# A GLA-plus-mixer kernel with a hand-written instruction order: another order and another buffer assignment

## The chip, the cores and the metric

The kernel runs on one core of one Trainium2 chip. The metric is the device time of one execution in microseconds. All times below are of that kind, or are spans and durations out of one profiled execution.

## The reference

Two layers follow each other. The first is a gated linear recurrence over 768 positions for 4 batches and 8 heads of width 48; the second is a mixer over tokens and then over channels, on the 4 x 768 x 384 result. Inputs and output are float32.

```python
for t in range(S):                      # S = 768, D = 48
    state = alpha[:, :, t, :, None] * state + einsum('bhd,bhe->bhde', k[:, :, t], v[:, :, t])
    y[:, :, t] = einsum('bhd,bhde->bhe', q[:, :, t], state)
x = y.transpose(0, 2, 1, 3).reshape(B, S, H * D)          # 4 x 768 x 384
h = maximum(x.transpose(0, 2, 1) @ w_tok1, 0) @ w_tok2    # 768 -> 256 -> 768
u = x + h.transpose(0, 2, 1)
out = u + maximum(u @ w_ch1, 0) @ w_ch2                   # 384 -> 1536 -> 384
```

## The kernel before

**The recurrence** is cut into twelve pieces n = 0 to 11 of 256 positions, three per batch (n = 3b + k). A piece holds its positions as 128 partitions x 2 slots, for all heads. Per piece: four loads of 384 KB (`ld_at` alpha, `ld_kt`, `ld_qt`, `ld_vt`); the logarithm of alpha (`ln`, from n = 3 on split in `P`, `ln1`, `lnP`, `r1`); its running sum by matmuls with a triangle (`cum`, `cumw`); the exponentials `E` and `IE`; the scaled keys and queries (`kk`, `kl` = keys x IE into `pkk`; `qq`, `ql` = queries x E into `pkq`, with `k0a` and `q0r` ahead of them from n = 3 on); a bf16 copy of v (`vb`) and the swapped halves of it (`vs0`, `vs1`); the transposes of keys and queries (for n < 6 on TensorE, `trk`, `trq`, with copies `evk`, `evq` out of PSUM; for n >= 6 by DMA transposes `dk`, `dq`, and a rearranging copy `pq`); the scores `G0`, `G1` and their masks; the outer products `K`, the state (`s0`, `sa`, `sm`), and the output `ia`, `ib`, `y0`, `y1`, copied out as `x0`, `x1`. From n = 3 on, `K` reads keys whose halves were exchanged between partitions by copies `ka`, `kb` (into `kt`) and `kc` (within `pkk`).

**The mixer** of batch b: `t1` (12 matmuls of 384 columns) and its ReLU `ht`; `t2` (6 groups of 2) and u = x + t2 (`u`); the transpose of u (`up` and copies `ut` on TensorE for batches 0 and 1, DMA transposes `ux` for 2 and 3); the first channel product `c1` (24 groups of 3 matmuls of 384 columns) with 24 ReLUs `rt`; the second, `c2` (6 rows x 4 groups of 3 matmuls), the sum `o` with u, and the store `st`. The 16 weight pieces (`ldw`, 384 KB each) come in on the same SyncE queue as the inputs and are cast to bf16 by `cw`.

**What sets the order.** A `Plan` object holds 946 named operations with what each writes, reads and waits for. A string `ORDER` lists them all, and the letter behind each name is its engine: t TensorE (PE), s ScalarE (ACT), v VectorE (DVE), g GpSimd (POOL), y SyncE (SP). Operations are emitted in the order of that list, so each engine's queue is the list's subsequence with its letter. A second string, `BUFS`, gives each value, when it is first met, a buffer out of its class (20 input buffers `in`, 8 PSUM banks `ps`, 20 `rt`, 4 `o` and so on). Waits follow from this: an instruction waits for its inputs and for the last user of the buffer that it writes.

```python
"in": 20, "la": 2, "lf": 2, "E": 3, "IE": 2, "pkq": 2, "pkk": 3, "vb": 3,
"tpk": 4, "tpq": 2, "gtm": 2, "tmp": 2, "ss": 4, "kt": 1, "x": 9, "ht": 3, "u": 4, "ut": 1, "rt": 20, "o": 4,
```

Operations marked `port` (products and casts between SBUF buffers: `P`, `k0a`, `q0r`, `kk`, `kl`, `qq`, `ql`, `vb`, `vs`, `ka`, `kb`, `kc`, `pq`, `cw`, and `sm` from n = 3 on) take turns between VectorE and GpSimd: where such an operation follows one on the other of the two engines in `ORDER`, it waits for it (function `shared`).

```python
if last and last[0] != e:
    self.tc.add_manual_dep(i.ins, last[1].ins.name, ...)
```

At the start, 25 matmuls on zeros (names `f1_`, `f3_`: one or three of 512 columns) stand ahead of the operation that they are named for. Lines that matter below: L604 recurrence matmuls and fillers, L805 `t1`, L810 `t2`, L821 `up`, L829 `c1`, L834 `c2`; L800 and L802 ReLUs on ACT and DVE; L697 copies on ACT, L698 copies on DVE and POOL; L720 masks; L589 `P`, L645 `k0a`, L649 `q0r`, L653 scaled keys and queries, L771 `sm`; L545 input loads, L677 DMA transposes of keys and queries, L585 stores.

Of the kernel before, what the change touches and what calls it, by code (L numbers as in the profile page):

```python
# [380 lines left out]
vs0_1g f3_G12t G0_2t G1_2t mask0_1v ldw_wt10y vs1_1g sm0_2v cw_wt10g t1_0_0_0t t1_0_0_1t ld_at3y P3g ldw_wt11y
cw_wt11g mask0_2v ia1t y0_1t ib1t t1_0_1_0t y1_1t ia2t lnP3s cum3t t1_0_1_1t y0_2t ld_kt3y x0_1s t1_0_0_2t ib2t
mask1_2v y1_2t ldw_wt20y t1_0_1_2t x1_1s t1_0_0_3t t1_0_1_3t IE3s x0_2v k0a3v t1_0_1_4t ldw_wt21y t1_0_0_4t x1_2s
t1_0_1_5t cw_wt20v ln13s kk3g kl3g t1_0_0_5t ht_0_0s cw_wt21s ht_0_1v t2_0_2t u_0_2v t2_0_1t u_0_1v ld_at4y P4g lnP4s
ldw_wc13y cw_wc13g t2_0_0t t2_0_3t t2_0_4t t2_0_5t u_0_0v up_0_0t ka3g kb3g u_0_3v up_0_1t ldw_wc11y trk3t cum4t
ut_0_1s IE4s E3s r13s E4s u_0_4v u_0_5v up_0_2t ldw_wc10y cw_wc10g ut_0_0v c1_0_7_0t c1_0_6_0t ut_0_2v c1_0_6_1t evk3v
rt_0_6_0s ld_qt3y kc3s cw_wc11v qq3v c1_0_7_1t rt_0_7_1s c1_0_1_0t c1_0_0_0t rt_0_0_0v ln14s r14s ld_vt3y vb3s
c1_0_3_0t c1_0_3_1t c1_0_1_1t c1_0_2_1t c1_0_2_0t q0r3g rt_0_6_1v rt_0_3_1v rt_0_7_0s rt_0_2_0s ql3g trq3t rt_0_3_0s
vs0_3g rt_0_1_1v rt_0_1_0v vs1_3g K3t s0_3v sa1_3v c1_0_0_1t ldw_wc14y cw_wc14g c1_0_8_1t c1_0_8_0t ldw_wc12y evq3s
ld_qt4y G0_3t rt_0_2_1s G1_3t cw_wc12g c1_0_4_0t q0r4g ql4g rt_0_0_1v ldw_wc15y cw_wc15s rt_0_8_1v mask0_3v qq4g  # L390
c1_0_9_1t rt_0_9_1s c1_0_11_1t c1_0_9_0t rt_0_9_0s rt_0_8_0v c1_0_11_0t ld_kt4y mask1_3v kk4g c1_0_5_1t trq4t k0a4v
kl4v c1_0_4_1t c1_0_5_0t rt_0_11_1s rt_0_4_0s ldw_wc20y cw_wc20s ldw_wc21y rt_0_11_0s evq4v trk4t rt_0_4_1s ld_at5y
cw_wc21g c2_0_2_0t P5g sm1_3g ka4g rt_0_5_0s c2_0_4_0t rt_0_5_1s ldw_wc22y kc4g cw_wc22s lnP5s evk4v G1_4t G0_4t
ld_vt4y vb4g mask1_4v ln15s r15s ib3t c1_0_10_0t rt_0_10_0v y1_3t c2_0_4_1t mask0_4v c2_0_2_1t c1_0_10_1t c2_0_1_0t
kb4s vs1_4s ldw_wc24y cw_wc24s vs0_4g x1_3v K4t y0_3t ldw_wc23y x0_3s cum5t IE5s E5s c2_0_1_1t cw_wc23g c2_0_4_2t
sa0_4v sm0_4v sa1_4v ia4t y0_4t ld_at6y ln16s t1_1_0_0t r16s P6g c2_0_1_2t sm1_4v c2_0_2_2t ldw_wc25y cw_wc25v x0_4s
c2_0_0_0t c2_0_0_1t rt_0_10_1s c2_0_4_3t lnP6s cum6t E6s ib4t IE6s ld_qt5y q0r5v qq5v c2_0_2_3t y1_4t x1_4s trq5t
evq5s ld_kt5y k0a5v kk5v o_0_2v c2_0_1_3t o_0_1v ld_vt5y trk5t kc5s evk5v c2_0_0_2t c2_0_0_3t o_0_4v G1_5t ld_at7y
mask1_5v ld_kt7y G0_5t P7g t1_1_0_1t c2_0_5_0t c2_0_5_1t vb5s ld_at8y ld_vt7y ia5t mask0_5v vs0_5s lnP7s ld_kt6y k0a7g
K5t sa0_5v c2_0_5_2t t1_1_0_2t sm0_5v P8g c2_0_5_3t t1_1_1_0t y0_5t t1_1_1_1t x0_5v t1_1_1_2t ib5t vs1_5s y1_5t x1_5s  # L400
c2_0_3_0t t1_1_1_3t t1_1_1_4t st_0_2y t1_1_0_3t t1_1_0_4t t1_1_1_5t t1_1_0_5t ht_1_0s cum7t IE7s c2_0_3_1t ht_1_1v
t2_1_0t u_1_0v t2_1_1t u_1_1v E7s t2_1_2t u_1_2v t2_1_3t u_1_3v c2_0_3_2t t2_1_4t u_1_4v t2_1_5t up_1_0t k0a6g ln17s
# [490 lines left out]
```

## Time and profile before

| | before |
|---|---|
| median of 3 runs | 164.17 us (163.75 to 164.42) |
| profiled execution: its time, its span | 164.12 us, 162.4 us |
| PE busy | 153.8 us (95%), 1598 matmuls |
| DVE busy | 112.4 us (69%), 200 instructions |
| ACT busy | 98.5 us (61%), 184 instructions |
| POOL busy | 80.4 us (50%), 95 instructions |
| HBM read, written | 25.17 MB, 4.72 MB |

The span runs from the first to the last instruction of the profiled execution; its time is 1.7 us longer. Busy time counts a matmul from its start to its modelled end, and matmuls overlap, so a hole in TensorE's row is shorter in the profile than the time that it costs.

### The profile page before, as it was taken

Reading aid. Unit: us, or ns where it says so; the run is one execution under the profiler, and the core shown is the slowest. Engines: PE = TensorE matmul, PEld = TensorE weight load, DVE = VectorE, ACT = ScalarE, POOL = GpSimd, SP = SyncE. Lnnn points to the kernel's source line nnn. Section 1 sums busy time; section 2 is a strip of 40 time slices with the busy share of each in tenths; the row PEclk is TensorE's granted clock in tenths of the full one; section 3 lists DMA queues with packets and bytes.
Section 4 is the critical chain, followed back from the end, with each engine's and each line's share of the span. In section 5 each row is a group of like instructions: output and inputs, shape, how many; then the busy total and the mean of one; then the engine's idle time right before and its main releaser. Section 6 shows DMA issues by size and latency. Waiting matters only on the chain.

```text
span 162.4 us, 4056 instructions
## 1 busy us (share of the span) xinstructions
PE 153.8 (95%) x1598; PEld 97.3 (60%) x1598; DVE 112.4 (69%) x200; ACT 98.5 (61%) x184; POOL 80.4 (50%) x95
## 2 busy tenths in 40 slices
PE   7988798999999999999899999999999999999992
PEld 2556465665666766756556675666667666666661
DVE  4287987988988994958896859767876544551232
ACT  3897576887889774899999794518532101437000
POOL 4066575769694048997279998658320000000000
PEclk9999999999999999999999999999999999999999
DMA  5999999999999999899999999999531063101134
GB/s 135 325 325 304 262 350 358 301 315 359 354 281 259 274 299 326 182 251 224 258 251 166 270 161 311 154 239 246 69 145 52 0 154 77 59 4 48 48 145 145
DMA packets 76322, 34.46 MB, mean 212 GB/s; under 512 B 68112, under 2 KB 76304, under 8 KB 76304
## 3 DMA queue, kind: packets, MB, share of 16 engines
q1 hardware_dynamic: 75152, 32.64, 79.4%
q10 hardware_dynamic: 1152, 1.57, 2.6%
q8 instruction: 12, 0.20, 0.5%
q14 instruction: 6, 0.05, 0.1%
HBM read 25.17 MB, written 4.72 MB: 184 GB/s over the span
## 4 chain that ended last, share of the span: by engine, by line
PE 66%; ACT 10%; DMA 7%; POOL 5%; DVE 5%; issue 4%; SPq 1%; DVEq 0%; POOLq 0%; ACTq 0%
PE ps L834 26%; PE ps L829 19%; PE ps L604 14%; DMA in<-in_alpha_dram 7%; PE ps L805 3%; PE ps L810 3%; ACT rt L800 3%; DVE gtm L720 2%; POOL vb L698 1%; POOL pkk L653 1%; PE ps L666 1%; DVE u L814 1%; SPq L677 1%; POOL in L589 1%; ACT lf L592 1%
## 5 line engine op out<-in xcount | busy, mean ns | idle before, releaser
L834 PE MATMUL ps<-wc,rt 128*128 128x384 bf16 (+2 forms) x300 | 53.2, 319 | 0.0
L829 PE MATMUL ps<-ut,wc 128*128 128x384 bf16 x288 | 50.0, 326 | 0.1
L800 ACT ACTIVATE rt<-ps 128x384 bf16<-128x384 f32 x55 | 24.7, 493 | 24.9 <-PE ps L829 20.3
L829 PEld LDWEIGHTS <-wc 128*128 128x128 bf16 x288 | 27.3, 98 | 18.1 <-POOL wc L698 0.5
L834 PEld LDWEIGHTS <-rt 128*128 128x128 bf16 x300 | 27.1, 98 | 15.8 <-issue 0.2
L720 DVE TENSOR_TENSOR gtm<-ps,mk 128x1024 bf16<-128x1024 f32 x24 | 28.6, 1217 | 2.6 <-PE ps L604 1.2
L802 DVE TENSOR_SCALAR rt<-ps 128x384 bf16<-128x384 f32 x41 | 21.5, 551 | 8.7 <-PE ps L829 8.7
L838 DVE TENSOR_TENSOR o<-ps,u 128x384 f32<-128x384 f32 (+2 forms) x25 | 13.0, 534 | 12.9 <-PE ps L834 10.8
L653 POOL TENSOR_TENSOR pkq<-in,E 128x384 bf16<-128x384 f32 (+1 forms) x12 | 16.8, 1409 | 6.5 <-DVE ss L771 2.9
L653 POOL TENSOR_TENSOR pkk<-in,IE 128x384 bf16<-128x384 f32 (+1 forms) x10 | 14.0, 1411 | 4.2 <-DVE wt L698 2.2
L698 POOL CAST vb<-in 64x384 bf16<-64x384 f32 (+1 forms) x15 | 9.1, 608 | 9.2 <-DVE pkk L653 6.5
L814 DVE TENSOR_TENSOR u<-ps,x 128x384 bf16<-128x384 f32 x24 | 11.8, 548 | 2.7 <-PE ps L810 2.7
L589 POOL TENSOR_TENSOR in<-in 128x384 f32<-128x384 f32 x9 | 8.9, 998 | 8.9 <-DMA in<-in_alpha_dram 5.0
L697 ACT CAST x<-ps 128x384 bf16<-128x384 f32 x16 | 7.5, 476 | 9.0 <-PE ps L604 8.9
L697 ACT CAST vb<-in 64x384 bf16<-64x384 f32 (+1 forms) x20 | 12.3, 622 | 1.0 <-POOL vb L698 0.6
L805 PE MATMUL ps<-x,wt 128*128 128x384 bf16 x48 | 10.9, 326 | 0.1
L649 POOL TENSOR_TENSOR in<-in,lf 128x384 f32<-128x384 f32 x8 | 8.0, 996 | 4.0 <-DMA in<-in_q_dram 2.1
L810 PE MATMUL ps<-ht,wt 128*128 128x384 bf16 x48 | 8.9, 326 | 0.6 <-ACT ht L800 0.6
L604 PE MATMUL ps<-zs 128*128 128x512 bf16 x25 | 8.4, 466 | 1.1 <-DVE zs L507 1.1
L604 PEld LDWEIGHTS <-tpk 48*64 48x64 bf16 (+1 forms) x288 | 5.8, 102 | 4.7 <-issue 3.1
L768 DVE TENSOR_TENSOR tmp<-ps,ss 128x384 f32<-128x384 f32 x12 | 6.7, 557 | 2.8 <-PE ps L604 0.8
L604 PE MATMUL ps<-vb,gtm 128*128 128x48 bf16 x192 | 8.2, 183 | 0.4 <-DVE gtm L720 0.4
(92 smaller groups left out, 208.1 us busy)
## 6 DMA issues: line engine op xcount, KB each, us to landing
in<-in_alpha_dram SPq DMA_DIRECT2D x12, 384.0 KB, 5.2
in<-in_q_dram SPq DMA_DIRECT2D x12, 384.0 KB, 4.8
in<-in_k_dram SPq DMA_DIRECT2D x12, 384.0 KB, 4.9
in<-in_v_dram SPq DMA_DIRECT2D x12, 384.0 KB, 4.9
in<-in_moe_w_ch_dram SPq DMA_DIRECT2D x12, 384.0 KB, 6.4
out_dram<-o SPq DMA_DIRECT2D x15, 192.0 KB, 2.0
in<-in_moe_w_tok_dram SPq DMA_DIRECT2D x4, 384.0 KB, 5.9
out_dram<-o ACTq DMA_DIRECT2D x8, 192.0 KB, 1.9
```

The source lines that it names most:

```text
L604: return self.pe.matmul(out, lhsT=lhsT, rhs=rhs, start=start, stop=stop, skip_group_check=True)
L653: self.shared(self.eng[e].tensor_tensor(self.t(dst)[:, c : c + z, :, 0:D], self.t(src)[:, :, c : c + z, :].rearrange("p h s d -> p s h d") ...
L697: return self.act.copy(d, s)
L720: self.nc.vector.tensor_tensor(self.t(gtm)[:, hf, :, :], self.pair(gp).rearrange("p a (j t) -> p (a j) t", t=128), bass.AP(tensor=m.tensor ...
L800: self.act.activation(d, s, AF.Relu)
L802: self.nc.vector.tensor_scalar_max(d, s, 0.0)
L805: self.pe.matmul(self.bank(bank)[:, 0:HD], lhsT=self.wt1[:, kc, m * 128 : m * 128 + 128], rhs=self.t(x), start=(kc == 0), stop=(kc == NS - 1))
L810: self.pe.matmul(self.bank(bank)[:, 0:HD], lhsT=self.wt2[:, kc, i * 128 : i * 128 + 128], rhs=self.t(hts[kc]), start=(kc == 0), stop=(kc = ...
L814: self.nc.vector.tensor_tensor(self.t(u)[:, i % 3], self.bank(bank)[:, 0:HD], self.t(x), ALU.add)
L829: self.pe.matmul(self.bank(bank)[:, 0:HD], lhsT=self.wc1[:, kc, mc * 128 : mc * 128 + 128], rhs=self.t(ut)[:, 3 * half : 3 * half + 3, kc, ...
L834: self.pe.matmul(self.bank(bank)[:, 0 : cz - ca], lhsT=self.t(rts[mc][0])[:, i * 128 : i * 128 + 128], rhs=self.wc2[:, mc, ca:cz], start=( ...
L838: self.nc.vector.tensor_tensor(self.t(o)[:, ca:cz], self.bank(bank)[:, 0 : cz - ca], self.t(u)[:, i % 3, ca:cz], ALU.add)
```

## The change

`ORDER` and `BUFS` are replaced; nothing else is. The same 946 operations are issued, 393 of them on TensorE with the same 1598 matmuls. Engines change for some: ScalarE goes from 191 to 195 (stores on its queue among them, 8 before and 11 now), VectorE from 182 to 188, GpSimd from 83 to 76, SyncE from 97 to 94. Batch 0's pieces, their loads (alpha of piece 4 ahead of piece 3, for one) and the weight pieces come in another sequence. The first lines of the two tables, cut:

```diff
 ORDER = """
-f1_trq1t ld_at0y f1_trq0t ln0s ld_at1y ln1s f3_trk0t f3_cumw1t f3_cumw0t cumw0t cumw1t Et0s E0s IE0s IE1s E1s ld_qt0y
+f1_trq1t f1_trq0t f3_cumw0t ld_at0y f3_trq1t ld_at1y ln0s ln1s cumw0t Et0s f3_cumw1t f1_K0t cumw1t IE0s ld_kt0y kl0v
...
 BUFS = """
-6 0 2 1 14 0 3 4 0 0 0 1 1 13 0 0 17 1 0 7 1 3 1 4 0 2 1 0 7 4 15 0 4 2 0 2 2 7 6 1 0 9 0 2 0 1 19 4 2 0 18 0 7 1 2 6
+1 0 6 3 16 0 1 0 0 2 4 1 1 14 0 12 6 3 0 4 0 17 1 3 2 15 1 6 0 4 1 0 2 13 0 1 1 0 2 2 1 6 10 1 0 4 11 1 6 0 9 2 6 4 0
...
```

Three places are shown as rows of the queues. The first is the halves' exchange for piece 6. Before, ScalarE does the last copy of it (`pkk_96` onto itself) behind the cast of a v tile and an exponential:

```order
L800 ACTIVATE rt_136<-ps 128x384
L800 ACTIVATE rt_134<-ps 128x384
L697 CAST vb_100<-in_76 128x768
L634 ACTIVATE IE_91<-ps 128x384
L697 COPY pkk_96<-pkk_96 64x8x48
L592 ACTIVATE lf_86<-in_70 128x384
L800 ACTIVATE rt_142<-ps 128x384
```

Now VectorE does it (the keys of piece 6 are in `pkk_97` here) and one of the two copies into `kt`, between two sums `o`:

```order
L698 COPY ut_132<-ps 128x768 x2
L838 TENSOR_TENSOR o_155<-ps,u_129 128x384
L698 COPY pkk_97<-pkk_97 64x8x48
L698 COPY kt_98<-pkk_97 64x8x48
L838 TENSOR_TENSOR o_154<-ps,u_128 128x384
L762 TENSOR_TENSOR ss_112<-ps,E_88 128x384
```

So two copies of piece 6 left ScalarE's queue and now take a turn of the port between VectorE and GpSimd.

The second place is GpSimd's queue for pieces 6 and 7. Before, it runs `P` of piece 8, `k0a` and the keys of 6, both steps of the queries of 6, the keys of 7 and both steps of its queries, and a half of v of 6:

```order
L589 TENSOR_TENSOR in_68<-in_68 128x8x48
L645 TENSOR_TENSOR in_77<-in_77,in_72 128x8x48
L653 TENSOR_TENSOR pkk_96<-in_77,IE_91 128x16x48
L649 TENSOR_TENSOR in_71<-in_71,lf_87 128x8x48
L653 TENSOR_TENSOR pkq_94<-in_71,E_89 128x16x48
L653 TENSOR_TENSOR pkk_97<-in_66,IE_92 128x16x48
L649 TENSOR_TENSOR in_74<-in_74,lf_86 128x8x48
L653 TENSOR_TENSOR pkq_93<-in_74,E_88 128x16x48
L698 CAST vb_100<-in_76 64x384
```

Now, it runs `P` of piece 8, v of 6, the keys of 7, both steps of the queries of 6 and of 7, `P` of piece 9, a state product, a half of v of 7, and the exchange copy of piece 7:

```order
L589 TENSOR_TENSOR in_81<-in_81 128x8x48
L698 CAST vb_100<-in_78 128x768
L653 TENSOR_TENSOR pkk_95<-in_65,IE_92 128x16x48
L649 TENSOR_TENSOR in_71<-in_71,lf_87 128x8x48
L653 TENSOR_TENSOR pkq_94<-in_71,E_88 128x16x48
L649 TENSOR_TENSOR in_76<-in_76,lf_86 128x8x48
L653 TENSOR_TENSOR pkq_93<-in_76,E_89 128x16x48
L589 TENSOR_TENSOR in_79<-in_79 128x8x48
L771 TENSOR_TENSOR ss_115<-tmp_111,E_88 128x384
L698 CAST vb_99<-in_75 64x384
L698 COPY pkk_95<-pkk_95 64x8x48
```

The keys of piece 6 left this queue, and the exchange copy of piece 7, which ScalarE did before, came in.

The third place is SyncE's queue of loads around alpha of piece 7. Before (alpha of piece 6, a weight, q, k and v of piece 5, alpha of piece 7 into `in_69`, k of 7, alpha of 8):

```order
L545 DMA in_72<-in_alpha_dram 128x8x96
L569 DMA in_73<-in_moe_w_ch_dram 128x2x384
L545 DMA in_83<-in_q_dram 128x8x96
L545 DMA in_76<-in_k_dram 128x8x96
L545 DMA in_65<-in_v_dram 128x8x96
L545 DMA in_69<-in_alpha_dram 128x8x96
L545 DMA in_66<-in_k_dram 128x8x96
L545 DMA in_68<-in_alpha_dram 128x8x96
```

Now (k, q and v of piece 5, q, alpha and k of piece 6, k of 7, alpha of 7 into `in_80`, alpha of 8):

```order
L545 DMA in_74<-in_k_dram 128x8x96
L545 DMA in_68<-in_q_dram 128x8x96
L545 DMA in_70<-in_v_dram 128x8x96
L545 DMA in_71<-in_q_dram 128x8x96
L545 DMA in_76<-in_alpha_dram 128x8x96
L545 DMA in_72<-in_k_dram 128x8x96
L545 DMA in_65<-in_k_dram 128x8x96
L545 DMA in_80<-in_alpha_dram 128x8x96
L545 DMA in_81<-in_alpha_dram 128x8x96
```

Alpha of piece 7 was the 42nd transfer of 384 KB in the queue and is the 45th now.

More of the change, by code (lines that the diff above doesn't have):

```diff
@@ L381 @@
[L381 to L390, printed above, removed]
@@ new lines @@
+r13s u_0_5v ln14s ut_0_1v up_0_2t ut_0_2v c1_0_3_0t c1_0_2_0t ld_kt3y k0a3g c1_0_2_1t rt_0_2_1v c1_0_1_0t kk3v
+c1_0_0_1t c1_0_3_1t c1_0_7_0t kl3v ka3v rt_0_1_0v trk3t rt_0_2_0s rt_0_3_1v c1_0_6_0t rt_0_6_0v ldw_wc14y cw_wc14s
+c1_0_8_0t r14s E4s kc3g ldw_wc15y cw_wc15s c1_0_8_1t c1_0_1_1t evk3v c1_0_11_0t kb3s ldw_wc12y cw_wc12s ld_qt3y q0r3v
+ld_vt3y qq3v ql3g c1_0_9_0t rt_0_9_0v rt_0_0_1s rt_0_7_0s rt_0_8_0s c1_0_5_1t c1_0_4_1t c1_0_6_1t vb3s vs0_3g
+c1_0_5_0t vs1_3s rt_0_1_1v rt_0_11_0s rt_0_4_1v ld_kt4y rt_0_5_1s kk4v k0a4v rt_0_3_0v trq3t c1_0_10_0t K3t s0_3v
@@ new lines @@
+rt_0_5_0s c1_0_11_1t c1_0_10_1t kl4g rt_0_8_1s ld_qt4y evq3s q0r4g c1_0_0_0t ldw_wc21y c1_0_7_1t sa1_3v G0_3t
+rt_0_10_0s rt_0_6_1s rt_0_11_1v G1_3t rt_0_7_1v qq4g kb4s c1_0_9_1t trk4t rt_0_0_0s cw_wc21s rt_0_9_1s mask0_3v
+ldw_wc24y ql4g trq4t rt_0_10_1s c1_0_4_0t mask1_3v y0_3t ldw_wc20y cw_wc20g c2_0_5_0t ldw_wc22y ib3t y1_3t evq4s
+rt_0_4_0v ld_at5y cw_wc24s x0_3v evk4v ln15s r15s cw_wc22g P5g ldw_wc23y cw_wc23g c2_0_4_0t c2_0_4_1t sm1_3g G1_4t
+G0_4t mask0_4v c2_0_1_0t c2_0_1_1t c2_0_1_2t ldw_wc25y cw_wc25v ld_vt4y vb4g ka4s mask1_4v c2_0_5_1t c2_0_5_2t
@@ new lines @@
+q0r7g qq7g rt_1_5_0v P9g dk7y sa1_6v sm1_6g rt_1_11_1v c1_1_6_1t c1_1_11_0t c1_1_5_1t rt_1_5_1v cum8t ld_kt9y
+c1_1_10_0t rt_1_10_0v rt_1_4_0s rt_1_11_0v vs0_7s c1_1_3_1t c1_1_7_1t c1_1_2_1t c1_1_9_0t dq6y IE8s vs1_7g E8s
+rt_1_1_1s k0a8v q0r8v k0a9v rt_1_2_1v c1_1_3_0t c1_1_2_0t rt_1_2_0v kb7s ka7s c1_1_0_0t rt_1_0_0v rt_1_9_0s rt_1_3_1s
+dq7y lnP9s rt_1_3_0s rt_1_7_1s pq6s c1_1_9_1t kc7g K7t rt_1_9_1v sa0_7v cum9t c1_1_10_1t rt_1_10_1s c1_1_8_1t
+rt_1_6_1s c1_1_0_1t ld_at10y c2_1_1_0t ld_qt9y pq7s ld_vt8y kk8g st_0_4y dk8y E9s rt_1_8_1v sm0_7g sa1_7v c1_1_4_1t
@@ new lines @@
+rt_2_3_0s rt_2_8_0s G1_10t mask1_10v dq11y c1_2_11_1t rt_2_11_1v c1_2_9_0t vs1_11s sm1_10g c1_2_4_0t t1_3_1_1t
+t1_3_1_2t y1_10t c1_2_10_0t pq11v rt_2_10_1s st_1_2y K11t sa0_11v c2_2_4_0t c2_2_4_1t x1_10s rt_2_4_0s rt_2_10_0s
+G0_11t G1_11t mask0_11v mask1_11v t1_3_1_3t c2_2_4_2t c2_2_5_0t c2_2_5_1t sm0_11v ia11t y0_11t x0_11s c2_2_5_2t
+c1_2_11_0t rt_2_11_0s ib11t t1_3_0_0t t1_3_0_1t t1_3_0_2t y1_11t x1_11s t1_3_0_3t t1_3_0_4t t1_3_1_4t c2_2_2_0t
+t1_3_0_5t t1_3_1_5t rt_2_9_0v c2_2_5_3t c2_2_1_0t ht_3_1s ht_3_0v t2_3_2t t2_3_1t u_3_2v t2_3_0t u_3_0v t2_3_3t u_3_1v
```

100 lines of the change are left out of this document (45 added, 55 removed), and 20 rows, old and new, of the table BUFS.

## The prediction

> **What bounds it now.** I read the stretches first, cut at places of the mixer: the start up to batch 0's first channel product `c1`; from there to batch 1's first `c1`; the stretch in which pieces 6 to 8 are prepared; two more; the drain. Columns are the stretch, its length, then busy time of PE, PEld, DVE, ACT and POOL, the clock, DMA share and GB/s.
>
> ```profile
> 0.00:30.70 30.70, 26.51 (x334) 16.66 (x335) 22.06 (x50) 21.05 (x33) 17.39 (x31) 1.00 1.03 297
> 30.70:68.20 37.50, 37.33 (x384) 24.35 (x385) 31.74 (x51) 29.61 (x59) 24.87 (x29) 1.00 1.02 294
> 68.20:86.30 18.10, 17.12 (x155) 10.35 (x154) 14.47 (x26) 17.62 (x35) 13.14 (x11) 1.00 1.18 235
> 86.30:105.50 19.20, 19.13 (x306) 12.53 (x302) 14.59 (x21) 13.96 (x26) 16.96 (x19) 1.00 1.10 220
> 105.50:158.90 53.40, 53.40 (x427) 33.22 (x426) 28.93 (x52) 16.28 (x34) 8.06 (x8) 1.00 0.38 101
> 158.90:162.40 3.50, 0.27 (x10) 0.15 (x6) 0.62 (x2) 0.00 (x0) 0.00 (x0) 0.91 0.37 129
> ```
>
> TensorE is the bound: its idle time is 4.2, 0.2, 1.0, 0.1, 0 and 3.2 us. Both orders issue the same matmuls, so the time can only change by TensorE's holes. The middle hole is at three places; the timeline of TensorE shows them, the bracket being the idle time ahead and who ended it.
>
> ```profile
> 69.72 3.09 PE L829 MATMUL ps<-ut,wc 128*128 128x384 bf16 x18
> 73.03 0.33 PE L604 MATMUL ps<-vb,pkk 128*128 128x96 bf16 x4 [0.23 <-ACT pkk L697]
> ...
> 73.37 5.65 PE L829 MATMUL ps<-ut,wc 128*128 128x384 bf16 x33
> 79.51 0.33 PE L604 MATMUL ps<-vb,pkk 128*128 128x96 bf16 x4 [0.49 <-ACT pkk L697]
> ...
> 81.39 0.65 PE L829 MATMUL ps<-ut,wc 128*128 128x384 bf16 x3
> 82.31 0.64 PE L604 MATMUL ps<-tpq,tpk 48*64 48x128 bf16 x32 [0.26 <-ACT tpq L697]
> ```
>
> The brackets understate. Where nothing waits, 54 `c1` matmuls take 8.78 us, so one goes in each 0.163 us (a group of three in 0.488), although each is shown for 0.326:
>
> ```profile
> 135.74 8.78 PE ps L829 x54
> ```
>
> So 18 matmuls from 69.72 end their turn at 72.65, and `K6` began at 73.03: 0.38 lost. The same from 73.37 (33: 78.74 against 79.51) gives 0.77 ahead of `K7`, and from 81.39 (3: 81.88 against 82.31) 0.43 ahead of piece 6's scores. Together 1.58 us. Each was released by a copy at the end of a full ScalarE queue (17.6 of 18.1 us busy): the exchange copies of pieces 6 and 7 and the first rearranged query copy.
>
> ```profile
> 72.38 0.51 ACT L697 COPY pkk<-pkk 64x384 bf16<-64x384 bf16 x1
> ...
> 78.86 0.51 ACT L697 COPY pkk<-pkk 64x384 bf16<-64x384 bf16 x1
> ...
> 79.78 1.25 ACT L800 ACTIVATE rt<-ps 128x384 bf16<-128x384 f32 x3
> 80.89 2.58 ACT L697 COPY tpq<-tpk 128x1024 bf16<-128x1024 bf16 x2
> ```
>
> **The start: no change.** What the first `c1` waits for is the masks of batch 0, which end on VectorE at 24.03, and the first `c1` follows at 30.73:
>
> ```profile
> 4.12 0.84 ACT L598 ACTIVATE la<-in 128x768 bf16<-128x768 f32 x1 [2.04 <-DMA in<-in_alpha_dram]
> 8.16 1.02 DVE L653 TENSOR_TENSOR pkk<-in,IE 128x384 bf16<-128x384 f32 x2
> 10.26 1.97 POOL L653 TENSOR_TENSOR pkk<-in,IE 128x384 bf16<-128x384 f32 x2 [0.19 <-DMA in<-in_k_dram]
> 21.67 2.36 DVE L720 TENSOR_TENSOR gtm<-ps,mk 128x1024 bf16<-128x1024 f32 x2
> 30.73 5.52 PE L829 MATMUL ps<-ut,wc 128*128 128x384 bf16 x33
> ```
>
> In the new order I follow the chain by hand. Logarithm done 4.97; running sum and the first exponential to about 7.1; two key products on DVE (1.02) to 8.1; two query products on POOL (1.97) to 10.1; the v cast and two query products on DVE (1.6) to 11.7; piece 1's two key products on POOL (1.97) to 13.7; transpose and copy to 15.0; then DVE without a pause: five masks at 1.18 (half of 2.36) and six products at 0.5, 8.9, to 24.0. The masks end where they did. Behind them the last `t1` comes about 0.45 earlier, since nothing of piece 3 stands among the `t1`, so `c1` begins about 30.25; but piece 3's key transpose (8 matmuls, 0.45), done by then before, is still to come. Net 0. One price is unknown: no DVE cast of a v tile is in the trace. The two DVE casts of weights of that size average 0.753, a POOL one 0.823; I take 0.6, and the bounds for the start are -0.5 and +0.4.
>
> **Batch 0's channel stage: no change.** Before, little is lost (0.17 idle). In the new order ScalarE casts three weight pieces and a v tile between its ReLUs; I find it ready within 0.1 us of TensorE's wish at each reused PSUM bank, and one wait of 0.3 for piece 4's queries on POOL, one of 0.3 for a state product. Against that, the holes before around `K3`. Bounds -0.4 and +1.0.
>
> **Pieces 6 to 8: -1.5.** The 1.58 can go only if what now makes the operands is in time. These prices carry it:
>
> ```profile
> L653 POOL TENSOR_TENSOR pkq<-in,E 128x768 bf16<-128x768 f32 x6 | 10.9, 1820 | 3.3 <-DVE ss L771 2.9
> L589 POOL TENSOR_TENSOR in<-in 128x384 f32<-128x384 f32 x9 | 8.9, 998 | 8.9 <-DMA in<-in_alpha_dram 5.0 <-DVE ss L771 3.7
> L649 POOL TENSOR_TENSOR in<-in,lf 128x384 f32<-128x384 f32 x8 | 8.0, 996 | 4.0 <-DMA in<-in_q_dram 2.1 <-DMA in<-in_moe_w_ch_dram 1.6 <-ACT lf L601 0.3
> L771 POOL TENSOR_TENSOR ss<-tmp,E 128x384 bf16<-128x384 f32 x6 | 5.0, 834 | 2.3 <-DVE tmp L768 2.2
> L698 POOL CAST vb<-in 128x768 bf16<-128x768 f32 x5 | 4.1, 823 | 6.6 <-DVE pkk L653 6.5
> L653 DVE TENSOR_TENSOR pkk<-in,IE 128x768 bf16<-128x768 f32 x2 | 1.9, 957 | 0.2 <-POOL in L649 0.2
> L698 DVE CAST vb<-in 64x384 bf16<-64x384 f32 x1 | 0.4, 355 | 0.0
> 56.56 1.00 POOL L589 TENSOR_TENSOR in<-in 128x384 f32<-128x384 f32 x1 [4.82 <-DMA in<-in_alpha_dram]
> 63.26 0.33 PE L604 MATMUL ps<-la,u 128*128 128x384 bf16 x1
> ```
>
> Alpha of piece 7 was the 42nd load and POOL took it at 56.56, as it landed. As the 45th it lands three loads later: 3 x 0.393 MB at the 294 GB/s of that stretch is 4.0, so 60.5. VectorE then does `k0a`, `P` (about 0.5 each) and the keys of 6 (0.96), to about 62.8 with a product of its own in front. POOL follows: `P8`, v, keys of 7, both steps of queries 6, 0.998 + 0.823 + 1.82 + 0.996 + 1.82 = 6.5, to 69.3. Then the two exchange copies on DVE take their turn of the port. None such is in the trace: a DVE cast of that size took 0.355, the ACT copies 0.51; I take 0.36, the same engine, and get 70.0 (70.3 at the other end). `K6` is now wanted behind five `c1` groups where nine stood before: 72.65 less 4 x 0.488, and 0.3 for a running sum that now stands behind it: 70.4. In time by 0.4.
>
> `K7`: POOL goes on with queries 7, `P9`, a state product and a half of v (0.996 + 1.82 + 0.998 + 0.834 + 0.5 = 5.15, to 75.1), three DVE products (1.65, to 76.8) and the exchange copy (0.5): 77.3. Without the holes TensorE wants it at about 77.9. In time by 0.6. Piece 6's scores: ScalarE has ten operations between piece 8's running sum (done about 73.7) and the query copy, eight at the 0.38 spacing of the ReLU row above and two exchange copies at about 0.53, so the copy (half of 2.58) ends near 79.3; wanted 81.4. A last ReLU behind it comes 0.1 late. So 1.58 less 0.1.
>
> **From 86 us on: +0.4.** Between 86.3 and 105.5 nothing changes by my rows. After 105.5 TensorE had no hole, so this part can only lose. The new order puts batch 3's `c1` among batch 2's `c2`; most places have half a microsecond, but four (a query copy on DVE ahead of piece 11's scores, three sums `o` just ahead of a reused bank) have 0.1. I charge 0.1 each; bounds 0 and +1. The drain's operations are the same.
>
> **The sum:** 0 + 0 - 1.5 + 0.4 = -1.1. Against the profiled execution's own 164.12 us (a span of 162.4 and 1.7 around it; the median of the runs is 164.17) this is 163.0 us. About 0.5%, 0.8 us, is what a measurement of this kernel can tell from no change, so faster means below 163.3 and slower above 164.9.
>
> **The rivals.** *Another wait takes the holes' place.* The chain to `K6` and `K7` is one unbroken run on POOL with two turns of the port, and its margins are 0.4 and 0.6. If its hand-overs cost 0.2 each and the copies 0.5, or alpha of 7 lands 1 us later, both holes return: 1.1 us given back, 164.1. For it: POOL's means are flat, but every delay adds up, as nothing pauses. Against: before, its idle time there was 5 us.
>
> *Slower: the transfer of alpha 7 becomes the bound.* The running sum of piece 7 stood in TensorE's queue at 63.26, with the same work ahead of it now. New: landing 60.5, `k0a`, `P`, logarithm (about 0.5 each) to 62.4 or so; margin 0.9. It decides from a landing of 61.4 on; then TensorE, the keys of 6 and all of the POOL run are late alike. SyncE's queue is in order and each load waits for its buffer's last reader, so a late reader moves all loads behind it. Two and a half microseconds beyond the margin's end make 163.0 + 2.5 = 165.5. For it: POOL waited 4.82 us for this very transfer before. Against: the loads behind it run at a steady rate in the 30.7 to 68.2 row.
>
> *The clock at the start.* The fillers' weight loads show the clock: 0.43 apart, then 0.36 and 0.22, so the array went to full rate near 4.7.
>
> ```profile
> 4.02 0.15 PEld L604 LDWEIGHTS <-zs 128*128 128x128 bf16 x1 [0.28 <-issue]
> 4.45 0.15 PEld L604 LDWEIGHTS <-zs 128*128 128x128 bf16 x1 [0.28 <-issue]
> 4.81 0.10 PEld L604 LDWEIGHTS <-zs 128*128 128x128 bf16 x1 [0.21 <-issue]
> 5.03 0.48 PEld L604 LDWEIGHTS <-u 128*128 128x128 bf16 x3
> ```
>
> Eleven fillers stood ahead of the first running sum; now eight do. They end near 4.45, and TensorE idles until the logarithm's 4.97. If it is still at half rate then, the sum takes twice its 0.88 and all of the start chain slides: 163.0 + 0.9 = 163.9. [...] The trace's one release, 3.7 us after the first matmul, does not settle it.
>
> **How the numbers follow.** Forecast 0.42, first rival 0.26, slower 0.20, clock 0.12. The forecast's own spread, from its bounds, is about 162.0 to 163.8, and three quarters of it and more lie below 163.3: with a few hundredths from the other cases, faster 0.38. Same: the rest of the forecast, the first rival and the clock, 0.41. Slower 0.21. The range 162.0 to 165.5 leaves out about 0.1 on the slow side and less than that below.
>
> **What would show it.** Right: `K6` and `K7` without an idle bracket, the first `c1` near 30.3, idle time of the third stretch under 0.3. Wrong: a bracket at `K6` released by DVE's copy or POOL; piece 7's running sum released by ACT behind a DMA; weight loads of the first running sum 0.27 apart; holes in TensorE's row after 105.

## The result and the profile after

The changed kernel takes 162.3 us (median of 4 runs, 162.16 to 162.64) where the kernel before takes 164.16 beside it (163.75 to 164.42): 0.9901 of it, with an interval of 0.9874 to 0.9928. That is 1.9 us less; 163.0 was forecast. The profiled execution of the new order took 162.33 us with a span of 160.6, 1.8 below the old one's.

The stretches of the new order, cut at the first `c1` of batch 0 and of batch 1, and behind the last matmul (columns as in the prediction):

```profile
0.00:30.00 30.00, 26.07 (x326) 16.41 (x327) 21.19 (x49) 20.87 (x33) 15.73 (x30) 1.00 1.04 303
30.00:67.00 37.00, 36.97 (x388) 24.85 (x388) 32.42 (x55) 30.77 (x60) 22.65 (x27) 1.00 1.05 292
67.00:86.30 19.30, 18.84 (x203) 11.67 (x201) 15.57 (x27) 18.12 (x36) 15.71 (x15) 1.00 1.20 240
86.30:105.50 19.20, 19.12 (x271) 12.57 (x269) 17.15 (x28) 12.15 (x23) 12.58 (x14) 1.00 1.07 243
105.50:157.60 52.10, 51.98 (x418) 32.09 (x416) 26.52 (x50) 16.97 (x37) 5.75 (x5) 1.00 0.38 91
157.60:160.60 3.00, 0.00 (x0) 0.00 (x0) 0.18 (x2) 0.00 (x0) 0.00 (x0) 1.00 0.51 178
```

TensorE idles 3.9 us, then 0.03, 0.46, 0.08, 0.12 and the drain's 3.0. The holes of pieces 6 to 8 are gone but for one, ahead of `K7`; in TensorE's row the bracket is again the idle time and who ended it:

```profile
69.48 0.33 PE L604 MATMUL ps<-vb,pkk 128*128 128x96 bf16 x4
...
72.62 4.55 PE L829 MATMUL ps<-ut,wc 128*128 128x384 bf16 x27
77.62 0.34 PE L604 MATMUL ps<-vb,pkk 128*128 128x96 bf16 x4 [0.46 <-POOL pkk L698]
```

The 27 `c1` from 72.62 end their turn at 77.01 (27 x 0.1627), so `K7` lost 0.61.

Brackets understate, as the prediction says. So each kind of matmul was given the distance that it keeps where nothing waits (0.1627 for `c1`, `c2` and `t1`, 0.335 for the eight of a `K`, 0.57 for the 32 of a pair of scores of pieces 6 to 11, and so on), and what the distance from one operation's start to the next exceeds this was summed over all 1598 matmuls. In us:

| part, by the mixer's places | lost, old order | lost, new order | change | forecast |
|---|---|---|---|---|
| up to the first `c1` | 8.15 | 7.90 | -0.25 | 0 |
| batch 0's channel stage, up to batch 1's first `c1` | 1.64 | 0.93 | -0.7 | 0 |
| pieces 6 to 8, up to piece 6's scores | 1.70 | 0.96 | -0.75 | -1.5 |
| the rest, up to the last matmul | 1.21 | 1.20 | 0 | +0.4 |
| sum | 12.7 | 11.0 | -1.7 | -1.1 |

In this execution the forecast's total was near, its parts were not. The experiments ask why `K7` still waits, why the copies' engines matter, and which of the parts hold in other executions. In the edited kernels the line numbers are four lower. Comparisons leave disturbed runs out, so a ratio is not always that of the two medians beside it.

### The profile page after: what moved, and what is told of

Same layout as the page of the kernel before. It is cut to its first block, busy times and chain, and to the rows that moved or that the text cites. A ratio compares the mean times of both kernels' runs of the same rounds, so it can differ in the third digit from the quotient of the medians.

```text
span 160.6 us, 4046 instructions
## 1 busy us (share of the span) xinstructions
PE 153.0 (95%) x1598; PEld 97.6 (61%) x1598; DVE 113.0 (70%) x206; ACT 98.9 (62%) x185; POOL 72.4 (45%) x88
## 4 chain that ended last, share of the span: by engine, by line
PE 74%; DVE 7%; DMA 6%; POOL 4%; ACT 3%; issue 3%; SPq 0%; DVEq 0%; POOLq 0%
PE ps L829 27%; PE ps L834 25%; PE ps L604 10%; PE ps L810 5%; PE ps L805 5%; DMA tpk<-pkk 4%; DMA in<-in_alpha_dram 3%; PE ps L666 2%; DVE gtm L720 2%; DVE pkk L653 1%; POOL pkq L653 1%; POOL pkk L653 1%; DVE pkq L653 1%; DVE ss L762 1%; DVE o L838 1%
## 5 line engine op out<-in xcount | busy, mean ns | idle before, releaser
L834 PE MATMUL ps<-wc,rt 128*128 128x384 bf16 (+2 forms) x300 | 54.2, 319 | 0.0
L829 PE MATMUL ps<-ut,wc 128*128 128x384 bf16 x288 | 51.9, 326 | 0.2 <-ACT IE L634 0.2
L800 ACT ACTIVATE rt<-ps 128x384 bf16<-128x384 f32 x58 | 26.4, 490 | 22.9 <-PE ps L829 22.6
L802 DVE TENSOR_SCALAR rt<-ps 128x384 bf16<-128x384 f32 x38 | 20.2, 552 | 13.1 <-PE ps L829 13.1
L653 POOL TENSOR_TENSOR pkq<-in,E 128x384 bf16<-128x384 f32 (+1 forms) x11 | 15.0, 1375 | 9.6 <-DVE pkk L653 5.5
L698 POOL CAST vb<-in 64x384 bf16<-64x384 f32 (+1 forms) x19 | 11.4, 604 | 11.5 <-DVE pkq L653 5.3
L653 POOL TENSOR_TENSOR pkk<-in,IE 128x768 bf16<-128x768 f32 (+1 forms) x8 | 12.1, 1513 | 6.6 <-DVE in L645 3.6
L697 ACT CAST vb<-in 64x384 bf16<-64x384 f32 (+1 forms) x16 | 9.8, 610 | 0.3
L697 ACT COPY tpq<-ps 128x1024 bf16<-128x1024 bf16 x6 | 7.8, 1308 | 2.6 <-PE ps L666 2.6
L604 PE MATMUL ps<-tpq,tpk 48*64 48x128 bf16 (+1 forms) x288 | 8.4, 219 | 0.1
```

The source lines that it names most:

```text
L604: return self.pe.matmul(out, lhsT=lhsT, rhs=rhs, start=start, stop=stop, skip_group_check=True)
L653: self.shared(self.eng[e].tensor_tensor(self.t(dst)[:, c : c + z, :, 0:D], self.t(src)[:, :, c : c + z, :].rearrange("p h s d -> p s h d") ...
L697: return self.act.copy(d, s)
L800: self.act.activation(d, s, AF.Relu)
L802: self.nc.vector.tensor_scalar_max(d, s, 0.0)
L829: self.pe.matmul(self.bank(bank)[:, 0:HD], lhsT=self.wc1[:, kc, mc * 128 : mc * 128 + 128], rhs=self.t(ut)[:, 3 * half : 3 * half + 3, kc, ...
```

## The experiments

**The new order again.** Two controls, unchanged, beside the other kernels.

> The new order unchanged, a control beside the next kernels. Theory (the array leaves half rate at a moment that differs from execution to execution; the four runs of the new order so far had it early): the runs spread from 162.2 to about 165, median 163.2 to 163.6, ratio to before 0.994 to 0.997. Rival (the array's release does not differ between these executions, the edits cost what their runs were above 162.3): median 162.2 to 162.6 again, ratio 0.990.

> The new order unchanged, beside the kernels of this call. Theory and rival alike: 162.2 to 162.8, ratio to before 0.989 to 0.992.

Measured: 162.45 (6 runs, 161.77 to 164.67; ratio 0.9889, 0.9850 to 0.9928) and 162.97 (7 runs, 162.26 to 163.8; 0.9918, 0.9881 to 0.9955). So the first result stands. The theory that its four runs were lucky by about a microsecond falls on the first control's ratio, at most 0.9928 where it wants 0.994 or more, though the runs spread as it said. The second control's interval reaches into that theory, and its median lies 0.2 above the range expected. Executions of the same kernel differ in where they lose, too: in the first control's profiled execution `K7` follows the 27 `c1` without a hole (72.85 + 4.39 = 77.24):

```profile
72.85 4.55 PE L829 MATMUL ps<-ut,wc 128*128 128x384 bf16 x27
77.24 0.34 PE L604 MATMUL ps<-vb,pkk 128*128 128x96 bf16 x4
```

**Whose hole is it at `K7`?** VectorE's, GpSimd's and SyncE's rows of the first profiled execution, in that order:

```profile
74.98 0.56 DVE L645 TENSOR_TENSOR in<-in,in 128x384 f32<-128x384 f32 x1 [0.65 <-POOL vb L698]
...
76.38 0.56 DVE L645 TENSOR_TENSOR in<-in,in 128x384 f32<-128x384 f32 x1 [0.38 <-DMA in<-in_k_dram]
```

```profile
77.06 0.50 POOL L698 COPY pkk<-pkk 64x384 bf16<-64x384 bf16 x1 [2.12 <-ACT rt L800]
```

```profile
68.39 2.53 SPq L677 DMA_TRANSPOSE tpk<-pkk  x1
70.96 0.58 SPq L545 DMA_DIRECT2D in<-in_k_dram  x1
```

The exchange copy of piece 7 on GpSimd starts at 77.06 after 2.1 us of idle time. The releaser that the row infers is a ReLU, but the order says otherwise: the copy takes its turn of the port behind `k0a` of piece 9 on VectorE, and that waited for the keys of piece 9, issued at 70.96 behind a transpose that held SyncE's queue for 2.5 us. In the first control the same product ran at 76.01 without a bracket, the copy at 76.68, and `K7` lost nothing; in the second the load landed at 76.74, the product waited 0.05 for it, and `K7` lost 0.16. Three kernels try this.

The first moves the product:

```diff
-k0a8v q0r8v k0a9v rt_1_2_1v ... c1_1_9_1t kc7g K7t rt_1_9_1v
+k0a8v q0r8v rt_1_2_1v ... c1_1_9_1t kc7g k0a9v K7t rt_1_9_1v
```

> The new order with one operation moved: k0a of piece 9 on VectorE goes from ahead of three ReLUs to behind the exchange copy kc7 on GpSimd. Theory (the hole that is left at K7 is a load: the keys of piece 9 land at 76.36, k0a9 on VectorE waits for them, and kc7 on GpSimd waits for k0a9 by the turn of the port): kc7 runs near 76.1 to 76.6, the ReLU that frees K7's second bank near 76.0 to 76.5, TensorE wants K7 at 77.0, so the 0.62 us ahead of K7 go: 161.7 against 162.3. Rival (GpSimd's chain itself is late, or the later keys of piece 9 open a hole of the same size at K8 or K9): 162.3.

Measured: 163.44 (12 runs, 162.39 to 164.78; 0.9962, 0.9932 to 0.9992). No gain. TensorE's row and GpSimd's:

```profile
77.13 0.33 PE L600 MATMUL ps<-vb,pkk 128*128 128x96 bf16 x4
...
81.21 0.88 PE L600 MATMUL ps<-tpq,tpk 48*64 48x128 bf16 x31 [0.19 <-DVE tmp L764]
```

```profile
76.13 0.50 POOL L694 COPY pkk<-pkk 64x384 bf16<-64x384 bf16 x1 [1.18 <-ACT rt L796]
77.95 1.82 POOL L649 TENSOR_TENSOR pkk<-in,IE 128x768 bf16<-128x768 f32 x1 [1.32 <-DVE in L641]
79.73 0.83 POOL L767 TENSOR_TENSOR ss<-tmp,E 128x384 bf16<-128x384 f32 x1
```

The copy runs at 76.13 and `K7` has no hole, as the theory has it. But the keys of piece 8 now wait for the moved product's turn of the port, the state product behind them ends at 80.56, VectorE's next one frees the bank of the scores, and those lose 0.67 (82.02 less 80.78 less their 0.57). The hole moved along the chain. That fits the profiled execution, which took 162.39 as the rival has it; the median is a microsecond above that, and what cost it is not shown.

The second moves it further, behind `sa1_7` too:

```diff
-k0a8v q0r8v k0a9v rt_1_2_1v ... kk8g st_0_4y dk8y E9s rt_1_8_1v sm0_7g sa1_7v
+k0a8v q0r8v rt_1_2_1v ... kk8g st_0_4y dk8y E9s rt_1_8_1v sm0_7g sa1_7v k0a9v
```

> The new order with k0a of piece 9 moved further back: behind the exchange copy of piece 7, the keys of piece 8, the state product sm0_7 and VectorE's sa1_7. Theory (after the move of k0a9 alone the hole of 0.6 went from K7 to the scores of piece 6, because the keys of piece 8 and sm0_7 on GpSimd stood behind k0a9's turn of the port): both holes go, TensorE loses 0.5 to 0.6 less between the first c1 and the end than in the new order, 0.6 below the new order at an equal start. Rival (a third wait stands behind: the queries of piece 8, 0.5 later): 0 to 0.2.

Measured: 162.81 (10 runs; 0.9926, 0.9894 to 0.9958), within the controls. Both holes are gone, and a third wait has come, as the rival has it though at another place: the running sum of piece 10 starts 1.31 behind the `c2` ahead of it, where 0.49 is the distance. Its bank is freed by a sum `o` on VectorE, and that stands behind a query product that waited 1.28 for its turn of the port. The scores at 91 lose another 0.5 to the next sum `o`. VectorE's row, then TensorE's:

```profile
87.67 0.56 DVE L645 TENSOR_TENSOR in<-in,lf 128x384 f32<-128x384 f32 x1 [1.28 <-POOL pkk L694]
```

```profile
88.44 0.65 PE L830 MATMUL ps<-wc,rt 128*128 128x384 bf16 x3
89.75 0.32 PE L600 MATMUL ps<-la,u 128*128 128x384 bf16 x1 [0.66 <-DVE o L834]
```

The third leaves all computing where it is and issues the load ahead of the transpose:

```diff
-... P9g dk7y sa1_6v sm1_6g ... cum8t ld_kt9y c1_1_10_0t
+... P9g ld_kt9y dk7y sa1_6v sm1_6g ... cum8t c1_1_10_0t
```

> The new order with one load moved: the keys of piece 9 go ahead of the DMA transpose of piece 7's keys in SyncE's queue, so they are issued near 68.4 instead of 70.96 (70.05 in the control) and land near 74.5 instead of 76.36 (74.79). Nothing else is moved. Theory (the hole at K7 is this load's landing, which comes late in some executions only; k0a9 then holds the exchange copy of piece 7 by the turn of the port): no hole at K7, 0 to 0.6 per execution, median 0.1 to 0.4 below the new order. Rival (the transpose, 0.6 later, now holds the exchange copy and K7): a hole of the same size stays, median equal or above.

Measured: 162.39 (6 runs, 161.45 to 163.15; 0.9885, 0.9842 to 0.9927). `k0a9` runs without a bracket, and `K7` starts 4.40 behind its 27 `c1` (at 72.79), which is their due:

```profile
75.96 0.55 DVE L641 TENSOR_TENSOR in<-in,in 128x384 f32<-128x384 f32 x1
```

```profile
77.19 0.34 PE L600 MATMUL ps<-vb,pkk 128*128 128x96 bf16 x4
```

So the cause of `K7`'s hole is the load, through VectorE's product and the turn of the port: moving the product takes the hole away, though the load lands at 76.07 and 77.03 there, and so does the load that lands early (73.85 here). That the place in the queue alone decides isn't shown, for the first control's load came behind the transpose and was in time. The gain can't be told from nothing: its interval holds both controls' ratios. In its profiled execution 0.34 of it was lost again at 111, where TensorE, early, met a sum `o` that waited for a store out of its buffer; that `o` was at 110.55 in the new order's first execution too. VectorE's row and TensorE's:

```profile
110.64 0.56 DVE L834 TENSOR_TENSOR o<-ps,u 128x384 f32<-128x384 f32 x1 [1.18 <-DMA out_dram<-o]
```

```profile
111.25 1.14 PE L825 MATMUL ps<-ut,wc 128*128 128x384 bf16 x6 [0.17 <-DVE o L834]
```

**The copies' engine and their place.** First the old order, with its three late copies moved. The exchange copy of piece 6 goes ahead of the v cast in ScalarE's queue (its transpose keeps its place in SyncE's), the last one of piece 7 to VectorE, the query copy ahead of two ReLUs:

```diff
-c1_1_8_0t vb7s vs1_7g dk6y IE8s rt_1_1_0v kc6s ld_at9y
+c1_1_8_0t dk6y kc6s vb7s vs1_7g IE8s rt_1_1_0v ld_at9y
...
-vs0_7s q0r8g ... rt_1_6_1s kc7s rt_1_0_0s K7t
+vs0_7s kc7v q0r8g ... rt_1_6_1s rt_1_0_0s K7t
...
-dq7y rt_1_1_1s rt_1_5_1s pq6s c1_1_3_1t
+dq7y pq6s rt_1_1_1s rt_1_5_1s c1_1_3_1t
```

> The old order with its three late operand copies taken from their places in ScalarE's queue: kc6 goes ahead of the v cast and the exponential of piece 8, kc7 goes to VectorE ahead of q0r8, pq6 goes ahead of two ReLUs. Theory (the holes at K6, K7 and G0_6 are made by ScalarE's queue): the idle brackets at K6 and K7 go and the one at G0_6 is under 0.2, which is 1.0 to 1.5 of the 1.58 us: 163.0 against 164.2. Rival (another wait stands right behind and takes the holes' place, as the first recorded rival has it): 164.0 to 164.2.

Measured: 164.89 (12 runs; 1.0028, 0.9997 to 1.0059). Not faster:

```profile
72.63 0.33 PE L600 MATMUL ps<-vb,pkk 128*128 128x96 bf16 x4
...
73.86 5.04 PE L825 MATMUL ps<-ut,wc 128*128 128x384 bf16 x30 [0.24 <-ACT rt L796]
78.75 0.33 PE L600 MATMUL ps<-vb,pkk 128*128 128x96 bf16 x4
...
80.90 0.65 PE L830 MATMUL ps<-wc,rt 128*128 128x384 bf16 x3 [0.64 <-DVE rt L798]
...
82.62 0.88 PE L600 MATMUL ps<-tpq,tpk 48*64 48x128 bf16 x31 [0.41 <-DVE tmp L764]
```

`K6` and `K7` start without a hole (as the theory says), and the time comes back at 73.9, 80.9 and 82.6: a late ReLU on ScalarE, a late one on VectorE, a late state product on VectorE (as the rival says). Moving three copies to better places does not make the gain; the new order moves ReLUs, products and loads with them.

Then the new order with piece 6's two copies back on ScalarE, at the same place of the list:

```diff
-c1_1_1_0t rt_1_1_0s kc6v kb6v K6t
+c1_1_1_0t rt_1_1_0s kc6s kb6s K6t
```

> The new order with the two exchange copies of piece 6, kc6 and kb6, back on ScalarE at the same place in the list. Theory (the engine of these copies decides): VectorE did the two in 0.55 us, ScalarE takes 2 x 0.51 from 69.16, so the second half of K6 starts near 70.2 instead of 69.7 and the ReLUs behind are 0.5 to 1.0 late: 162.8 against 162.3. Rival (the order alone mattered, ScalarE has room here): 162.3.

Measured: 163.47 (12 runs, 162.97 to 164.13; 0.9964, 0.9938 to 0.9990), by the ratios 0.5 to 0.75% above the controls. ScalarE's rows and TensorE's:

```profile
70.66 0.49 ACT L796 ACTIVATE rt<-ps 128x384 bf16<-128x384 f32 x1 [0.52 <-PE ps L825]
71.18 0.51 ACT L693 COPY pkk<-pkk 64x384 bf16<-64x384 bf16 x1
```

```profile
71.74 0.34 PE L600 MATMUL ps<-vb,pkk 128*128 128x96 bf16 x4 [1.11 <-ACT pkk L693]
72.27 0.34 PE L600 MATMUL ps<-vb,kt 128*128 128x96 bf16 x4 [0.19 <-ACT kt L693]
```

The direction is the theory's, the size in the rows more than twice its 0.5: 1.3 ahead of `K6` and 0.4 within it. That each copy takes 0.51 instead of 0.26 is the smaller part. On ScalarE they stand behind a ReLU that waits for the last `c1` ahead of `K6`, so TensorE waits for a ReLU of what it has just done, and then for two copies. On VectorE they are free of that. The rows carry this, the ratio less so: 0.9962 was measured with `k0a` of piece 9 moved, too, whose rows have no such loss.

**The slower rival.** Alpha of piece 7 is put behind two other loads:

```diff
-ld_kt7y ld_at7y ... ld_at8y ... ld_vt6y
+ld_kt7y ld_at8y ld_vt6y ld_at7y ...
```

> The new order with the loads of alpha of piece 8 and of v of piece 6 moved ahead of alpha of piece 7, so that this one lands two loads later, near 63.2 instead of 59.44. Theory (the recorded slower rival's mechanism and point: late from a landing of 61.4 on, and then the keys of piece 6 and all of GpSimd's run are late alike): 1.8 to 2.9 us late at K6, 164.1 to 165.2. Rival (slack along the chain takes most of it): 162.3 to 162.8.

Measured: 165.1 (12 runs, 163.91 to 167.75; 1.0048, 1.0012 to 1.0083), 1.3 to 1.6% above the controls. ScalarE's rows and TensorE's:

```profile
65.03 0.52 ACT L588 ACTIVATE lf<-in 128x384 f32<-128x384 f32 x1 [2.33 <-DMA in<-in_alpha_dram]
65.45 0.46 ACT L693 CAST x<-ps 128x384 bf16<-128x384 f32 x1
```

```profile
65.97 0.65 PE L801 MATMUL ps<-x,wt 128*128 128x384 bf16 x3 [1.94 <-ACT x L693]
```

The load landed at 65.0, and TensorE lost 2.1 us in one hole. So a late load does cost what the rival said, but the first to suffer is not the running sum: the first logarithm of piece 7 waits at the head of ScalarE's queue, and behind it stands the last x of batch 1, for which `t1` waits. Take the 2.1 off the landing, and in this execution it decides from 62.9 on. But this execution was 2.0 late from the start on (its first `c1` came at 32.07, against 30.03). In the new order's first execution TensorE wanted the same x 2.0 earlier, so there a landing decides from about 60.9 on, where 61.4 was forecast. It landed at 59.4, 1.1 earlier than forecast: a margin of 1.5, and that is why the rival did not come.

**The clock at the start.** Three more fillers ahead of the first running sum, where eight leave TensorE idle for 0.51 us in the new order's first execution (the row is below). The author's estimate was that without this idle time the slowest runs, over 164, go and the median comes 0.2 to 0.6 lower. The edit:

```diff
-f1_trq1t f1_trq0t f3_cumw0t ld_at0y f3_trq1t ld_at1y ln0s ln1s cumw0t Et0s f3_cumw1t f1_K0t cumw1t
+f1_trq1t f1_trq0t f3_cumw0t ld_at0y f3_trq1t f3_cumw1t ld_at1y ln0s ln1s cumw0t Et0s f1_K0t cumw1t
```

> The new order with three more fillers, those of cumw1, ahead of the first running sum, 11 there as in the old order instead of 8. [...] Rival (the idle time does not matter): the same spread, and the first sum 0.1 to 0.6 later behind the fillers: median equal or up to 0.4 above.

Measured: 163.19 (12 runs, 161.65 to 164.57; 0.9897, 0.9861 to 0.9934). Nothing can be told from the controls, and the spread stays: the estimate of a gain falls. What the start's rows show is that the half rate ends at another moment in each execution. The three wide matmuls of the first running sum take 0.65 at full rate; here they are in the new order's first execution, in the execution with the late alpha (the same start, eight fillers; both running sums), and with eleven fillers:

```profile
5.13 0.65 PE L604 MATMUL ps<-la,u 128*128 128x384 bf16 x3 [0.51 <-ACT la L598]
```

```profile
5.17 1.12 PE L600 MATMUL ps<-la,u 128*128 128x384 bf16 x3 [0.52 <-ACT la L594]
...
8.35 1.17 PE L600 MATMUL ps<-la,u 128*128 128x384 bf16 x3
```

```profile
5.72 1.17 PE L600 MATMUL ps<-la,u 128*128 128x384 bf16 x3
```

The first `c1` came at 30.03 in the first (the 0.5 us without work behind the eight fillers did no harm there), 30.04 to 30.6 in six others with this start, and 32.07 in the second execution shown, where the second running sum at 8.35 was still at half rate. With eleven fillers it came at 31.26. By the spacing of the weight loads (0.43 from filler to filler and 0.32 within a sum at half rate, 0.22 and 0.16 at full rate), full rate began between 4.0 and 5.1 us in the first, near 5.3 where `k0a` of piece 9 was moved, near 5.8 with ScalarE's copies, near 7.1 with eleven fillers, and near 10.5 in the one with 32.07. Of the three executions shown, the one with the later full rate has the later first `c1`. What sets that moment stays open; that the idle time between fillers and sum delays it is not shown: without that idle time it came near 7.1, with it earlier in three of these executions and later in one.

**Which part gains?** Three joins: one order up to a place, the other's remaining operations behind it. In outline:

```diff
-old order, whole
+old order up to K5 of piece 5, then what is left in the new order's sequence
+new order up to the first c1, then what is left in the old order's sequence
+old order up to the first c1, then what is left in the new order's sequence
```

> The old order up to the outer products of piece 5 (58 us), and from there the new order. By TensorE's spacing in the two traces the new order lost 0.25 us less up to the first c1, 0.7 less in batch 0's channel stage, 0.75 less around pieces 6 to 8 and the same after that. Theory (these parts add up): 0.75 below the old order, 163.4 against 164.15, with the old order's start. As recorded (the first two parts are worth nothing, pieces 6 to 8 1.5, the rest costs 0.4): 1.1 below, 163.05. Rival (the join or the buffers' change undo it): 164.0 or more.

> The new order up to the first c1 of batch 0 (30 us), and from there the old order. Theory (by TensorE's spacing the start gained 0.25 us in the profiled execution): 163.9 against 164.15. As recorded (start worth nothing): 164.15. Rival (the new start leaves other things undone, piece 3's key transpose among them, so that the old order behind it loses 0.5 or more): 164.6 or more.

> The old order up to the first c1 of batch 0, and from there the new order. Theory (by spacing the new order gained 0.7 in batch 0's channel stage, 0.75 around pieces 6 to 8, nothing after that, and these parts hold without the new start): 1.45 below the old order, 162.7. As recorded (batch 0's stage nothing, pieces 6 to 8 1.5, the rest 0.4 lost): 163.05. Rival (the join costs): 163.5 or more.

Measured: 167.12 (1.0178), 170.41 (1.0344) and 165.49 (1.0059, 1.0027 to 1.0092). All three are the rival's: the join costs more than the parts differ, so they say nothing on the table's parts. Why two of them are slow is worth seeing. In the third, TensorE waited 2.2 us at the join for the cast of a weight piece that the new order wants first, and then ran at half rate: TensorE's row at the join, and the stretch behind it, in which the clock is the number behind POOL's:

```profile
32.80 5.43 PE L825 MATMUL ps<-ut,wc 128*128 128x384 bf16 x22 [2.18 <-POOL wc L694]
```

```profile
33.00:36.00 3.00, 3.00 (x11) 1.44 (x10) 0.15 (x1) 1.11 (x3) 0.31 (x1) 0.50 0.99 260
```

Eleven matmuls in 3 us where 18 fit. By spacing the wait cost 2.3 and the half rate another 1.7 us. The second join has a wait of 3.2 us, and all its six runs a mean granted clock of 0.98, where the new order's first execution has 1.0. Of the third's twelve runs seven have 0.987 to 0.99 and five 1.0. From 28.82 up to its wait TensorE did little but transposes. The old order, the same up to there, has them without the wait, and its `c1` ran at full rate behind them (33 in 5.52); a wait of 2.2 us without them was not tried, so it stays open how short a wait alone would do.

## Why the prediction was right or wrong

**The total.** 162.3 lies in the range, and faster it is (below 163.3); of the chances given, same had a little more than faster. The forecast's mechanism holds in part. That the total came within 0.7 us of it is partly luck: in the first execution the 0.75 that pieces 6 to 8 gained less than forecast met a gain of 0.7 that was not forecast, and a loss of 0.4 that was forecast did not come.

**The start** (forecast 0, first `c1` at 30.25): 30.03, with piece 3's key transpose still to come as said, so 0.25 gained in the profiled execution, within its bounds. VectorE's chain is as worked out by hand: the last two masks end at 23.87 against 24.0, and the v cast, for which 0.6 was taken, took 0.56:

```profile
10.27 0.56 DVE L698 CAST vb<-in 128x768 bf16<-128x768 f32 x1 [0.39 <-POOL pkq L653]
...
21.52 2.35 DVE L720 TENSOR_TENSOR gtm<-ps,mk 128x1024 bf16<-128x1024 f32 x2
...
30.03 1.14 PE L829 MATMUL ps<-ut,wc 128*128 128x384 bf16 x6 [0.21 <-ACT IE L634]
```

**Batch 0's channel stage** (forecast 0, bounds -0.4 and +1.0): -0.7, and this is the step that failed. It read "little is lost (0.17 idle)" off the row of the stretch, although the prediction had just said that brackets understate and had used the distances for pieces 6 to 8. By distances the old order lost 1.64 there. At `K3` the rows of the old order, then of the new:

```profile
36.53 0.33 PE L604 MATMUL ps<-vb,pkk 128*128 128x96 bf16 x4
36.92 0.33 PE L604 MATMUL ps<-vb,kt 128*128 128x96 bf16 x4
37.09 1.87 PE L829 MATMUL ps<-ut,wc 128*128 128x384 bf16 x9
38.89 0.62 PE L604 MATMUL ps<-tpq,tpk 48*128 48x128 bf16 x16
```

```profile
39.69 0.33 PE L604 MATMUL ps<-vb,pkk 128*128 128x96 bf16 x4
39.86 0.33 PE L604 MATMUL ps<-vb,kt 128*128 128x96 bf16 x4
```

The halves of `K3` stand 0.39 apart before and 0.17 now, without any bracket (0.22 lost); the nine `c1` behind them took 1.80 to the scores where 1.46 is their due (0.34 lost). Such places add up. Which of the moved operations removes which of them was not tried by itself. How far the gain holds, the length of the stage shows, from batch 0's first `c1` to batch 1's: 37.0 us in the first execution, 37.0 to 37.2 in five others whose edits lie elsewhere, 37.5 in the one with ScalarE's copies and 37.9 in the second control, which lost 0.5 at 53, ahead of a key transpose that waited for VectorE. The old order's stage, unedited in the kernel with the three moved copies, came out 0.3 shorter than in its first execution. So of the 0.7 most is found again in most executions, but not in all.

**Pieces 6 to 8** (forecast -1.5): -0.75 in the first execution, but nearly the forecast in the controls. From batch 1's first `c1` to piece 6's scores the first execution took 14.25 us, the controls, in the same order, 13.57 and 13.72; that makes the gain 1.4 and 1.3 there. `K6` and piece 6's scores have no hole, as said. GpSimd's and VectorE's chain came nearly to the times worked out: the query product ended at 69.08 (69.3 forecast) and the two copies at 69.37 and 69.66 (70.0):

```profile
67.26 1.82 POOL L653 TENSOR_TENSOR pkq<-in,E 128x768 bf16<-128x768 f32 x1
```

```profile
69.11 0.26 DVE L698 COPY pkk<-pkk 64x384 bf16<-64x384 bf16 x1 [0.79 <-POOL pkq L653]
69.40 0.26 DVE L698 COPY kt<-pkk 64x384 bf16<-64x384 bf16 x1
```

The copy of piece 7 ended at 77.56 where 77.3 was forecast. But TensorE, which by the forecast would want it at 77.9, wanted it at 77.0, since it had gained 0.95 earlier. The margin of 0.6 was counted against a TensorE that was still late. And one step was missed: of VectorE's three products ahead of the copy's turn, the third waits for a load, which comes late in some executions.

**From 86 us on** (forecast +0.4): 0 in the first execution. The kind of wait was right: the sum `o` ahead of a reused bank is what cost 0.34 at 111 when the load was moved, where TensorE was earlier.

**The rivals.** Another wait takes the holes' place: partly, by a load and not by GpSimd's unbroken run. In the experiments on `K7` and in the old order with moved copies it is the whole story. Slower by alpha of piece 7: real in its size, 1.5 us away in its point where 0.9 was forecast. The clock: not in the first execution (the first sum's matmuls at full rate behind 0.5 us of idle time), in others yes, by 0 to 0.6 and once 2.0 at the first `c1`. How many fillers it takes no run shows: behind eight the first sum's three matmuls took 0.65 in one execution and 1.12 in another, behind eleven 0.65 in the old order's first execution and 1.17 with the three more in the new one.

## What to carry to other kernels

Measure a saturated engine's loss by the distance from start to start against the undisturbed one, in every stretch and not only where a bracket stands; the margins of later places are then to be counted against the earlier arrival, not the old one. A hole released by a copy may be a load three hand-overs back: look at the load's place in its queue first, for moving the waiting operation back moved the hole along the same chain here. Where nearly all holes are gone, an edit worth half a microsecond meets the next transfer and can't be told from the spread of executions.

## What the runs showed of the hardware

TensorE's half rate at the start ended at another moment in each execution: under one and the same start, between 4.0 and 5.1 us in the new order's first, with the first `c1` at 30.03, and near 10.5 in the run with the late alpha, with the first `c1` at 32.07. At half rate the first running sum's three matmuls took 1.12 to 1.17, at full rate 0.65. In the third join a wait of 2.2 us, behind transposes, was followed by half rate for about 3 us (clock 0.50 in the row), which cost 1.7 us on top of the wait. Behind a wait of 1.9 us in the profiled execution with the late alpha there was none, as `t1`'s three matmuls kept to 0.65. VectorE's copy of 64x384 between SBUF tiles took 0.26, half of the 0.51 and 0.50 that the same copy took on ScalarE and on GpSimd.
